# Splits moved to VectorE, a new order of slot widths, and exchanged operands in the last slot of a two-mixture kernel

## The chip, the core and the metric

The kernel runs on one core of a Trainium2 chip. Its engines work side by side and wait for one another through semaphores: PE (TensorE, matrix products), DVE (VectorE), ACT (ScalarE), POOL (GpSimd) and SP (SyncE, which here issues transfers); 16 DMA engines move data. The metric is the device time of one execution in microseconds (us). Unless another unit stands there, times in this text are us, and times within an execution count from the start of its span.

## The reference

All data are fp32. Attention comes first, then two mixtures of experts in a row, each with 1152 tokens of 512 values, 8 experts, and one expert per token:

```python
attn = softmax(scores + decay bias, causal) @ v      # 2 x 8 heads, 576 positions, 64 values
# mixture 1: at most `capacity` tokens of each expert are kept
e = argmax(x @ w_gate);  out = gate * (relu(x @ w1[e]) @ w2[e])      # w1 512x1024, w2 1024x512
# mixture 2: the same on that output, no capacity, a bias of each token's modality added to the logits
e = argmax(x @ w_gate2 + bias[modality]);  out = gate * (relu(x @ w1[e]) @ w2[e])
```

With the inputs used here the second mixture sends 550, 85 and 517 tokens to three experts and none to the others; the first mixture's experts 0 to 7 get 130, 137, 129, 143, 151, 156, 117 and 189.

## The kernel before

Attention fills about the first 110 us, with the routing of the first mixture at its end. The rest is a row of 13 *slots*. A slot is one expert with a fixed number of token columns. Slots 0 to 7 are the first mixture: slot 0 is expert 0 with 160 columns, slots 1 to 7 are the other experts sorted by their token count, and the widths stand in `WID` (160, 192, 168, 160, 152, 144, 136, 132). Slots 8 to 12 are the second mixture: 8 and 9 the expert with most tokens, 10 and 11 the second, with 276 columns each, and 12 a third with 92.

**Steps.** Every slot has eight steps j on PE, one for each 512 KB piece of weights. Steps 0 to 3 make 256 hidden rows each (`mul`, weights stationary, tokens moving), and relu follows in `fold` and `fold2`. Steps 4 to 7 make the output, 128 rows each; tiles of PSUM are shared by two steps. Where a slot is `native` (all of the first mixture but slot 1, and slot 12), PE multiplies fp32; each product shows as two matmul instructions in the trace. In slots 8 to 11 weights and tokens are split into a high and a low fp32r part and each product is three matmuls, hi x hi (L799), hi x lo (L800) and lo x hi (L801). Slot 1 is split too.

**Splits.** `split` (L697) makes the parts of a piece in two halves of 512 columns: ACT writes `hi`, and VectorE or GpSimd subtracts to give `lo`. With `alone` it is always VectorE; otherwise GpSimd takes the odd pieces. `stream` sets when a piece is fetched and split, in steps counted over all slots: in slot 8 (n = 8) piece i is fetched at step 57 + i and split at 60 + i, and used at 64 + i. Slot 10 is fetched and split later in the same manner; slots 9 and 11 use the parts of the slot before.

**The order around it.** PE's instructions are pinned in program order; SP's and POOL's transfers go out in order as well. `begin(prep(...))` starts a slot's transposes of gathered tokens (`ptx`, L760, to `xs` on ACT and VectorE) during the slot before, and `tail1` puts the routing of a finished slot among the next slot's products, at due times `T` (`TL` for slot 7) of a modelled clock: logits (`p`, `l`, `pl`, L882 to L894), the one-hot choice `oh` (L909), ranks by PE (`pr`, L912 to L915), then `place` (L154 to L183: `pos`, `colm`), the write of the slot's rows to DRAM (L941), and at the end the list of tokens by PE (`plist`, L944). For slot 7 this ends with `finished`: the list is read (L189) and POOL gathers the tokens of slot 9. `plan` (L1178 to L1194), which picks the experts of slots 10 to 12, comes between `place` and the write.

**The end.** Slot 12 goes the usual way: outputs with the 512 values on partitions are copied (`yT`, L843 and L844), turned by PE in two halves (`pty`, L866), scaled by ACT into `yr` (L867) and scattered to the output by POOL (L951), after a branch that would compute tokens left over (there are none here). `oi`, the rows to scatter to, comes from `tail2` (L962).

Of the kernel before, what the change touches and what calls it, by code (L numbers as in the profile page):

```python
# [26 lines left out]
GATE, TOK, BIAS = 512, 513, 520  # L27
NONE = 65536.0
OFF = {1: 2048, 2: 4096}
WID = [160, 192, 168, 160, 152, 144, 136, 132]  # L30
J1 = (N - H1) // H1 // W1 * W1 + W1 + 1
J2 = -(-(N + C2) // C2) * W2
J = {1: J1, 2: J2}
# [2 lines left out]
NSLOT2 = (N - E) // C2 + E  # L36
NS = {1: NOV, 2: NSLOT2}
PIECE = 1024
RAW = 8
T = 1.5, 2.3, 3.0, 5.6, 9.9, 2.0, 13.0  # L40
TL = 0.9, 1.7, 2.4, 4.6, 10.5, 2.0, 13.0
AWAKE = 22, 6, 16
DW = 128 + 2 * E
MID, PLACE = 32, 1.2
# [5 lines left out]
def shape_constants():  # L50

    import numpy as np

    p = np.arange(128).reshape(128, 1, 1)
    e = np.arange(E)
    tok = S * np.arange(B)[:, None] + 128 * np.arange(NT) - 64 + p
    tok[:, :, 0] = S * np.arange(B) + p[:, :, 0]
    t = {"io8": np.broadcast_to(e - E, (NT, E)), "tok": tok, "tok1": tok - OFF[1], "col": np.arange(E * J2),
         "row": C1 * np.arange(NCH)[:, None] + H1 * np.arange(W1) + p - OFF[2]}
    t["io8m"] = np.broadcast_to(t["io8"], (128, NT, E)).copy()  # L60
    t["io8m"][64:, 0, :] = 100
# [9 lines left out]
    t["width"] = np.array(WID[1:])  # L71
# [12 lines left out]

def build(tc, ctx, spots, tab, qk, v, s, wg, wa, cap, mod, wg2, mb, wb, out):
    nc = tc.nc
# [99 lines left out]

    def listed(dst, src, m):

        nc.vector.tensor_scalar_add(dst, src, float(OFF[m]))  # L189


    with ExitStack() as actx:
# [614 lines left out]
    def mul(k, j, lead=False):  # L807

        if j == 0:
            k.hs = (hidden1[:, 0:8 * k.c].rearrange("p (k c) -> p k c", k=8) if k.native else  # L810
                    hidden[:, 0:16 * k.c].rearrange("p (k s c) -> p k s c", k=8, s=2))
        if j == 4:
            k.yT = mp.tile([P, 4, k.c], F32, name="yT")
        if j < 4 or j % 2 == 0:
            k.ps = pg.tile([P, 2, 512], F32, tag="g", name="ps")
        if j < 4:
            for i in range(2):
                for kt in range(4):
                    if lead:
                        step(k)  # L820
                    product(k, k.ps[:, i], k.w[j], i * 512 + kt * P, k.xs[:, kt], kt == 0, kt == 3)
        else:
            late = j < 6 and k.two and 2 * k.c <= 512
            cuts = [(j, 0, 8)] if not late else [(4, 0, 4)] if j == 4 else [(5, 0, 4), (4, 4, 6), (5, 4, 6), (4, 6, 8), (5, 6, 8)]
            for d, k0, k1 in cuts:
                for kt in range(k0, k1):
                    if lead:
                        step(k)
                    product(k, k.ps[:, d % 2], k.w[d], kt * P, k.hs[:, kt], kt == 0, kt == 7)

# [28 lines left out]

    def back(k, yr, i):  # L860
        r0, r = k.rows[i]
        n = DM // P // (2 if k.last else 1)
        for d0 in range(0, DM // P, n):
            pt = pt_.tile([r, n * P], F32, tag="t", name="pty")
            for dt in range(n):
                pin(nc.tensor.transpose(pt[:, dt * P:(dt + 1) * P], k.yT[:, d0 + dt, r0:r0 + r], ident))  # L866
            nc.scalar.mul(yr[:r, i, d0 * P:(d0 + n) * P], pt, k.xc[:r, i, GATE:GATE + 1])  # L867
# [90 lines left out]
    def tail2(k):  # L958
        own = sm if k.last else mp
        oi = own.tile([H2, W2], I32, name="oi")  # L960
        with tc.issue_after(latest[nc.vector.engine]) if k.two else ExitStack():
            nc.vector.tensor_tensor(oi, k.xc[:, :, TOK], absent(k), op=ALU.add)  # L962
        yr = own.tile([H2, len(k.rows) if k.last else W2, DM], F32, name="yr2")
        for i in range(len(k.rows)):
            yield k.T[0] + (BRISK if k.next and k.next.last else T[5]) * i
            back(k, yr, i)
            if k.last:
                k.rest = lambda: put_rows(k, oi, yr, 0)
            else:
                put_rows(k, oi, yr, i)  # L970
# [70 lines left out]
    def when(t, f):  # L1041
        steps.setdefault(max(-(-t // 1), 0), []).append((t, f))

    def stream(n, k, src, known, pace=0.5):

        k.w, k.st = {}, {}

        def get(i):
            with tc.issue_after(k.hold()) if k.hold else ExitStack():
                k.st[i] = first[i] if n == 0 and i < len(first) else fetch(src, k.e, i)  # L1050

        def cut(i):
            k.w[i] = k.st.pop(i) if k.native else split(k.st.pop(i), i, alone=n < E)
        for i in range(8):
            tf = max(8 * n + i - FETCH, known + pace * i)
            ts = max(8 * n + i - SPLIT, tf + (2 if n < E else 3))
            when(tf, lambda i=i: get(i))
            when(ts, lambda i=i: cut(i))

    def ordered():  # L1060

        sq = [P, E - 1, E - 1]
        key = sm.tile([P, E - 1], F32, name="key")
        nc.vector.scalar_tensor_tensor(key, cnt1[:, 1:E], float(E), con["later"], op0=ALU.mult, op1=ALU.add)
        gt = sm.tile(sq, F32, name="gt")
        nc.vector.tensor_tensor(gt, key.unsqueeze(1).to_broadcast(sq), key.unsqueeze(2).to_broadcast(sq), op=ALU.is_gt)
        nth = sm.tile([P, E - 1], F32, name="nth")
        nc.vector.tensor_reduce(nth, gt, axis=AX.X, op=ALU.add)
        nc.vector.tensor_tensor(gt, nth.unsqueeze(1).to_broadcast(sq), col[:, 0:E - 1].unsqueeze(2).to_broadcast(sq),
                                op=ALU.is_equal)  # L1070
# [157 lines left out]
        nc.vector.tensor_tensor(done, done, full, op=ALU.min)  # L1228

    def finished():  # L1230
        listed(list2, pl2, 2)
        gather(seq[E + 1], pick(2, list2, seq[E + 1].cv))
        info["landed"] = nc.sync.dma_start(landed, seq[E + 1].xc[0:1, :, 0]).ins

    def assign():
# [7 lines left out]

    seq[E - 3].ranked = lambda: (choose(), close())
    seq[E - 3].listed = start
    seq[E - 1].placed = plan
    seq[E - 1].listed = finished
    at(E, KNOWN, assign)
    at(E + 1, 3, remain)
# [1 line left out]
    for i in range(5):  # L1251
# [16 lines left out]
    for n, k in enumerate(seq):  # L1268
# [13 lines left out]
            prev = (k, j)  # L1282
    finish()
    fold(*prev)
    for _ in k.tail():
        pass

    more_ = info["more"]
    latest.clear()
    with tc.If(more_ > 0):  # L1290
# [15 lines left out]
    k.rest()  # L1306


# [44 lines left out]
```

## Time and profile before

| | |
|---|---|
| median of 3 runs | 415.23 us (414.46 to 415.42) |
| the profiled execution | 418.99 us, its span 416.9 us |
| granted TensorE clock, mean | 0.99 of full speed |
| busy: PE, DVE, ACT, POOL | 398.1, 198.7, 179.6, 143.3 us |
| HBM read, written | 63.78, 10.51 MB |

The profile is one execution; it is 3.76 us longer than the median, of which 2.09 lie outside its span. An engine's busy time is the time in which it has an instruction at work; in a row of the timeline the first number is the start, the second the time that the merged instructions took, and brackets give the idle time ahead and what ended it.

### The profile page before, as it was taken

What the parts mean: (1) busy time and instruction counts of PE and PEld (TensorE: products, weight loads), DVE (VectorE), ACT (ScalarE), POOL (GpSimd) and SP (SyncE); (2) the same over time, 40 slices, a digit from 0 to 9 for tenths busy, and PEclk for the clock granted to TensorE, in tenths of its full rate; (3) what the DMA queues carried; (4) which work ended last, traced back from release to release, by engine and by line L of the source; (5) the groups of instructions that cost most, each with busy time, mean ns of one, the idle gap of its engine ahead of it and who ended that gap; (6) DMA issues with size and microseconds to landing.
All of it is one profiled execution on the core that took longest, in us unless ns stands there. A gap on an engine that the chain in (4) does not pass through costs nothing.

```text
span 416.9 us, 8847 instructions
## 1 busy us (share of the span) xinstructions
PE 398.1 (95%) x3177; PEld 367.2 (88%) x3177; DVE 198.7 (48%) x778; ACT 179.6 (43%) x472; POOL 143.3 (34%) x182
## 2 busy tenths in 40 slices
PE   8889999999889999999999999999999999999991
PEld 3778888888579999989899999989899999999990
DVE  8867779995715762314141423377721343221100
ACT  7979887896315632111211221266123454131221
POOL 4775876620281130302020202152556357030021
PEclk9999999999989999999999999999999999999997
DMA  4944896702138951767686878991059546010010
GB/s 175 313 134 156 313 380 231 266 4 85 45 110 300 375 179 39 237 205 263 203 265 211 270 239 270 266 343 53 8 170 375 169 152 190 36 31 27 0 51 23
DMA packets 30580, 74.64 MB, mean 179 GB/s; under 512 B 9196, under 2 KB 11628, under 8 KB 30526
## 3 DMA queue, kind: packets, MB, share of 16 engines
q1 hardware_dynamic: 24110, 66.72, 47.3%
q0 software_dynamic: 6336, 7.22, 6.6%
q8 instruction: 27, 0.44, 0.4%
q14 instruction: 27, 0.22, 0.2%
q10 hardware_dynamic: 80, 0.04, 0.0%
HBM read 63.78 MB, written 10.51 MB: 178 GB/s over the span
## 4 chain that ended last, share of the span: by engine, by line
PE 78%; DVE 9%; DMA 5%; ACT 3%; issue 1%; POOL 1%; POOLq 1%; SPq 0%; ACTq 0%; DVEq 0%
PE ps L791 30%; PE ps L799 6%; PE ps L800 6%; PE ps L801 6%; PE pt L365 5%; PE ps L365 5%; PE pty L866 3%; PE pb L365 3%; PE ps L795 2%; PE ptx L760 2%; PE px L365 2%; DMA wgid<-in_wg 2%; PE pa L365 2%; DVE lo L697 2%; PE p L882 1%
## 5 line engine op out<-in xcount | busy, mean ns | idle before, releaser
L791 PE MATMUL ps<-xn,st 128*128 128x160 f32 (+6 forms) x512 | 72.7, 296 | 0.4 <-ACT xn L779 0.4
L791 PE MATMUL ps<-hidden,st 128*128 128x160 f32 (+6 forms) x512 | 70.6, 292 | 0.0
L791 PEld LDWEIGHTS ps<-xn,st 128*128 128x128 f32 x512 | 67.8, 194 | 2.1 <-issue 1.0
L791 PEld LDWEIGHTS ps<-hidden,st 128*128 128x128 f32 x512 | 65.9, 190 | 0.6
L454 ACT ACTIVATE e<-sc,nmx 128x192 f32<-128x192 f32 (+4 forms) x80 | 44.7, 560 | 6.4 <-DVE sc L450 6.4
L844 DVE COPY yT<-ps 128x276 f32<-128x276 f32 (+7 forms) x24 | 8.5, 353 | 80.8 <-ACT yT L843 80.8
L721 POOL DMA_INDIRECT xc<-x,idx x14 | 15.0, 1074 | 75.1 <-DVE eq L904 54.7
L799 PE MATMUL ps<-xs,hi 128*128 128x276 f32 x128 | 38.4, 300 | 0.0
L799 PE MATMUL ps<-hidden,hi 128*128 128x276 f32 x128 | 38.2, 299 | 0.1
L843 ACT COPY yT<-ps 128x276 f32<-128x276 f32 (+7 forms) x24 | 7.6, 316 | 69.2 <-PE ps L791 39.3
L800 PE MATMUL ps<-hidden,hi 128*128 128x276 f32 x128 | 37.1, 289 | 0.2 <-DVE hidden L857 0.2
L800 PE MATMUL ps<-xs,hi 128*128 128x276 f32 x128 | 37.1, 290 | 0.0
L801 PE MATMUL ps<-xs,lo 128*128 128x276 f32 x128 | 37.1, 290 | 0.0
L801 PE MATMUL ps<-hidden,lo 128*128 128x276 f32 x128 | 37.1, 290 | 0.0
L365 PE MATMUL pt<-ident,e 128*128 128x128 f32 x240 | 35.4, 277 | 0.8 <-ACT e L454 0.6
L951 POOL DMA_INDIRECT out<-yr,oi x13 | 15.6, 1202 | 53.8 <-ACT yr L867 51.4
L697 POOL TENSOR_TENSOR lo<-st,hi 128x512 fp32r<-128x512 f32 x16 | 22.1, 1394 | 33.3 <-ACT hi L695 33.2
L450 DVE TENSOR_SCALAR_CACHE_REDUCE sc<-ps 128x192 f32<-128x192 f32 (+4 forms) x80 | 31.5, 417 | 2.0 <-ACT e L454 1.1
L365 PE MATMUL ps<-ka,qa 128*128 128x320 f32 (+2 forms) x96 | 30.0, 327 | 0.5 <-DVE sc L450 0.5
L695 ACT CAST hi<-st 128x512 fp32r<-128x512 f32 x48 | 27.7, 618 | 4.4 <-DMA st<-in_wa 3.5
L365 PEld LDWEIGHTS pt<-ident,e 128*128 128x128 f32 x240 | 26.1, 141 | 2.6 <-ACT e L454 0.8
L857 DVE SCALAR_TENSOR_TENSOR hidden<-ps,hidden 128x552 fp32r<-128x552 f32 x16 | 11.7, 731 | 29.7 <-ACT hidden L855 29.5
(292 smaller groups left out, 869.9 us busy)
## 6 DMA issues: line engine op xcount, KB each, us to landing
st<-in_wa SPq DMA_DIRECT2D x64, 512.0 KB
st<-in_wb SPq DMA_DIRECT2D x24, 512.0 KB
qkd<-in_qk SPq DMA_DIRECT2D x6, 1152.0 KB
y<-yr SPq DMA_DIRECT2D x8, 390.0 KB
vt<-in_v SPq DMA_DIRECT2D x8, 320.0 KB
qkd<-in_qk SPq DMA_DIRECT2D x4, 576.0 KB
out<-zrow SPq DMA_DIRECT2D x1, 2304.0 KB
x<-xrow SPq DMA_DIRECT2D x2, 768.0 KB
```

The costliest lines, as they stand in the source:

```text
L365: ins = op(*args, **kw)
L450: nc.vector.tensor_scalar(h.sc[t][:r, c0:c1], ps[:r, o0:o0 + c1 - c0], -0.125, low, op0=ALU.mult, op1=ALU.min, accum_out=h.nmx[t][:r])
L454: recent[:] = [nc.scalar.activation(ebuf[t, i][:r, :w], h.sc[t][:r, :w], AF.Exp, bias=h.nmx[t][:r], scale=-1.0, accum_out=rsum[:r, k.b, t, ...
L695: nc.scalar.copy(hi[:, c:c + h], st[:, c:c + h])
L697: eng.tensor_tensor(lo[:, c:c + h], st[:, c:c + h], hi[:, c:c + h].bitcast(F32), op=ALU.subtract)
L721: nc.gpsimd.indirect_dma_start(out=k.xc[:r, i, 0:rw], out_offset=None, in_=src, in_offset=bass.IndirectOffsetOnAxis(ap=idx[:r, i:i + 1], a ...
L791: pin(nc.tensor.matmul(out[:, 0:c], w[:, o:o + P], mv, start=first, stop=last, skip_group_check=True))
L799: pin(nc.tensor.matmul(out[:, 0:c], hi, mv[:, 0, :], start=first, stop=False, skip_group_check=True))
L800: pin(nc.tensor.matmul(out[:, 0:c], hi, mv[:, 1, :], start=False, stop=False, skip_group_check=True))
L801: pin(nc.tensor.matmul(out[:, 0:c], lo, mv[:, 0, :], start=False, stop=last, skip_group_check=True))
L866: pin(nc.tensor.transpose(pt[:, dt * P:(dt + 1) * P], k.yT[:, d0 + dt, r0:r0 + r], ident))
L951: put = nc.gpsimd.indirect_dma_start(out=out, out_offset=bass.IndirectOffsetOnAxis(ap=oi[:, i:i + 1], axis=0), in_=yr[:, i, :], in_offset= ...
```

## The change

1. The widths of slots 1 to 7 become 192, 136, 152, 132, 160, 144, 168 (ranks 0, 5, 3, 6, 2, 4, 1); each rank keeps its width.
2. The second weight matrix is packed in pieces of half of its 512 output values by half of its 1024 hidden rows. Steps 4 and 5 make the first 256 output rows, from hidden tiles 0 to 3 and 4 to 7, steps 6 and 7 the others. `late` cuts are gone.
3. Slot 8's pieces are split at steps 62 + i, all of them with VectorE; its `prep` begins at step 61, not 62.
4. `plan` is emitted after the gather of slot 9 and held behind the list; `TL[4]` is 9.4, not 10.5.
5. In slot 12's steps 4 to 7 the hidden tiles (128x92) are stationary and 256 weight columns move, so that tokens come out on partitions; ACT scales them straight into `yr`. Its `oi` is made at step 4, and its `tail2` is not run.

```diff
-WID = [160, 192, 168, 160, 152, 144, 136, 132]
+RANKED = [192, 168, 160, 152, 144, 136, 132]
+TURNS = [0, 5, 3, 6, 2, 4, 1]
+WID = [160] + [RANKED[r] for r in TURNS]
-TL = 0.9, 1.7, 2.4, 4.6, 10.5, 2.0, 13.0
+TL = 0.9, 1.7, 2.4, 4.6, 9.4, 2.0, 13.0
...
+        if j == 4 and k.last:
+            k.oi, k.yr = places(k), sm.tile([H2, 1, DM], F32, name="yrl")
...
-            late = j < 6 and k.two and 2 * k.c <= 512
-            cuts = [(j, 0, 8)] if not late else [(4, 0, 4)] if j == 4 else [(5, 0, 4), (4, 4, 6), (5, 4, 6), (4, 6, 8), (5, 6, 8)]
...
+            h, q = divmod(j - 4, 2)
+            if k.last:
+                for kt in range(4 * q, 4 * q + 4):
+                    for _ in range(2 if lead else 0):
+                        step(k)
+                    pin(nc.tensor.matmul(k.ps[:k.c, 0, 0:HD], k.hs[:, kt], k.w[j][:, kt % 4 * HD:kt % 4 * HD + HD],
+                                         start=kt == 0, stop=kt == 7, skip_group_check=True))
+                return
+            for k0 in range(4 * q, 4 * q + 4, 2 if j == 5 else 4):
+                for d in range(2):
+                    for kt in range(k0, k0 + (2 if j == 5 else 4)):
+                        if lead:
+                            step(k)
+                        product(k, k.ps[:, d], k.w[j], kt % 4 * HD + d * P, k.hs[:, kt], kt == 0, kt == 7)
...
+        if k.last and j > 3:
+            nc.scalar.mul(k.yr[:k.c, 0, HD * (j // 2 - 2):HD * (j // 2 - 1)], k.ps[:k.c, 0, 0:HD],
+                          k.xc[:k.c, 0, GATE:GATE + 1])
+            return
...
-            k.w[i] = k.st.pop(i) if k.native else split(k.st.pop(i), i, alone=n < E)
+            k.w[i] = k.st.pop(i) if k.native else split(k.st.pop(i), i, alone=n < E or i in late)
...
-            ts = max(8 * n + i - SPLIT, tf + (2 if n < E else 3))
+            ts = 8 * n + i - 2 if i in late else max(8 * n + i - SPLIT, tf + (2 if n < E else 3))
...
-        listed(list2, pl2, 2)
+        ready = listed(list2, pl2, 2)
         gather(seq[E + 1], pick(2, list2, seq[E + 1].cv))
+        with tc.issue_after(ready.ins):
+            plan()
...
-    seq[E - 1].placed = plan
...
-        at(n - 1, 7 if i == 1 else 6, lambda k=k, n=n: begin(prep(k, after=seq[n - 1])))
+        at(n - 1, (5, 7, 6, 6, 6)[i], lambda k=k, n=n: begin(prep(k, after=seq[n - 1])))
...
-            stream(n, k, wb, 8 * (E - 2) + 4) if i == 0 else stream(n, k, wb, 8 * (E + 1), 1)
+            stream(n, k, wb, 8 * (E - 2) + 4, late=range(8)) if i == 0 else stream(n, k, wb, 8 * (E + 1), 1)
```

## Rows read from the trace of the kernel before

**Rows 1.** The page: busy us of each engine (share of the span) x instructions.
```profile
PE 398.1 (95%) x3177; PEld 367.2 (88%) x3177; DVE 198.7 (48%) x778; ACT 179.6 (43%) x472; POOL 143.3 (34%) x182
```
**Rows 2.** Waits of PE: us in total, times, longest us.
```profile
PE ptx L760 <- DMA yc<-y,idx: 0.8, 1, 0.8
PE ptx L760 <- DVE xs L784: 0.7, 1, 0.7
...
PE pr L912 <- DVE oh L909: 0.4, 1, 0.4
```
**Rows 3.** Windows around the start of slot 8: us, busy by engine, clock, DMA, GB/s.
```profile
271.00:282.00 11.00, 10.31 (x93) 9.79 (x92) 8.33 (x20) 7.06 (x17) 5.49 (x4) 1.00 0.95 336
282.00:296.00 14.00, 13.73 (x113) 13.09 (x112) 11.81 (x41) 6.94 (x14) 6.04 (x4) 1.00 0.11 31
```
**Rows 4.** The chain that ended last, in slot 7: start, us, what.
```profile
265.62 5.39 DMA st<-in_wb
271.04 0.63 ACT hi L695
```
**Rows 5.** Timeline of PE, slots 7 and 8: start, us, instructions, idle before.
```profile
278.72 0.46 PE L760 MATMUL ptx<-ident,yc 92*128 92x92 f32 x3 [0.69 <-DVE xs L784]
...
288.57 0.17 PE L912 MATMUL pr<-oh,upper 96*96 96x16 bf16 x1
...
295.68 0.39 PE L944 MATMUL plist<-colm,pos 96*92 96x144 f32 x2 [0.27 <-DVE colm L183]
...
296.60 0.40 PE L799 MATMUL ps<-hidden,hi 128*128 128x276 f32 x1
...
299.46 0.39 PE L800 MATMUL ps<-hidden,hi 128*128 128x276 f32 x1 [0.19 <-DVE hidden L857]
...
307.37 0.30 PE L760 MATMUL ptx<-ident,yc 92*128 92x92 f32 x1 [0.75 <-DMA yc<-y,idx]
```
**Rows 6.** Timeline of POOL in slots 7 and 8.
```profile
273.54 2.93 POOL L697 TENSOR_TENSOR lo<-st,hi 128x512 fp32r<-128x512 f32 x2 [11.65 <-ACT hi L695]
...
291.47 2.06 POOL L697 TENSOR_TENSOR lo<-st,hi 128x512 fp32r<-128x512 f32 x1 [2.17 <-ACT hi L695]
294.00 1.31 POOL L697 TENSOR_TENSOR lo<-st,hi 128x512 fp32r<-128x512 f32 x1 [0.48 <-ACT hi L695]
```
**Rows 7.** Timeline of DVE in slots 7 and 8.
```profile
274.00 2.53 DVE L174 TENSOR_SCALAR pos<-ctab,pb__3761 96x92 fp32r<-96x92 f32 x2
...
277.03 1.28 DVE L697 TENSOR_TENSOR lo<-st,hi 128x512 fp32r<-128x512 f32 x2
...
284.90 0.22 DVE L894 TENSOR_REDUCE lg<-pl 96x16 f32<-96x64 f32 x1 [1.24 <-PE pl L889]
...
292.27 1.27 DVE L160 SCALAR_TENSOR_TENSOR pb__3993<-pb__3993,rank 96x2 f32<-96x2 f32 x1
293.58 0.56 DVE L174 TENSOR_SCALAR pos<-ctab,pb__3993 96x92 fp32r<-96x92 f32 x2
294.06 1.56 DVE L183 TENSOR_TENSOR colm<-ctab,hj 96x288 fp32r<-96x288 f32 x1
...
297.60 0.30 DVE L189 TENSOR_SCALAR list<-plist 92x144 int32<-92x144 f32 x1
```
**Rows 8.** Timeline of DVE in slot 1, whose splits VectorE makes alone.
```profile
142.59 0.22 DVE L894 TENSOR_REDUCE lg<-pl 96x16 f32<-96x64 f32 x1 [1.20 <-PE pl L889]
...
147.41 0.15 DVE L909 TENSOR_TENSOR oh<-ctab,mn 96x16 bf16<-96x16 f32 x1
```
**Rows 9.** Timeline: a native stretch of 168 columns, and the last slot's end.
```profile
168.30 3.67 PE L791 MATMUL ps<-xn,st 128*128 128x168 f32 x24
...
399.94 7.31 PE L791 MATMUL ps<-hidden,st 128*128 128x92 f32 x64
...
408.21 0.47 ACT L867 ACTIVATE yr<-pty,yc 92x256 f32<-92x256 f32 x1 [0.24 <-PE pty L866]
409.01 1.18 POOL L951 DMA_INDIRECT out<-yr,oi  x1 [8.23 <-ACT yr L867]
```

More of the change, by code (lines that the diff above doesn't have):

```diff
@@ L38 @@
 PIECE = 1024
+HD = DM // 2
 RAW = 8
 T = 1.5, 2.3, 3.0, 5.6, 9.9, 2.0, 13.0
-TL = 0.9, 1.7, 2.4, 4.6, 10.5, 2.0, 13.0
+TL = 0.9, 1.7, 2.4, 4.6, 9.4, 2.0, 13.0
 AWAKE = 22, 6, 16
@@ L70, in shape_constants @@
     t["base2"] = W[2] * np.arange(NS[2])
-    t["width"] = np.array(WID[1:])
+    t["width"] = np.array(RANKED)
+    t["turns"] = np.array(TURNS)
     t["later"] = E - 1 - np.arange(E - 1)
@@ L187, in listed @@
     def listed(dst, src, m):
-        nc.vector.tensor_scalar_add(dst, src, float(OFF[m]))
+        return nc.vector.tensor_scalar_add(dst, src, float(OFF[m]))
     with ExitStack() as actx:
@@ L811, in mul @@
                     hidden[:, 0:16 * k.c].rearrange("p (k s c) -> p k s c", k=8, s=2))
-        if j == 4:
+        if j == 4 and k.last:
+            k.oi, k.yr = places(k), sm.tile([H2, 1, DM], F32, name="yrl")
+        elif j == 4:
             k.yT = mp.tile([P, 4, k.c], F32, name="yT")
@@ L822, in mul @@
         else:
-            late = j < 6 and k.two and 2 * k.c <= 512
-            cuts = [(j, 0, 8)] if not late else [(4, 0, 4)] if j == 4 else [(5, 0, 4), (4, 4, 6), (5, 4, 6), (4, 6, 8), (5, 6, 8)]
-            for d, k0, k1 in cuts:
-                for kt in range(k0, k1):
-                    if lead:
-                        step(k)
-                    product(k, k.ps[:, d % 2], k.w[d], kt * P, k.hs[:, kt], kt == 0, kt == 7)
+            h, q = divmod(j - 4, 2)
+            if k.last:
+                for kt in range(4 * q, 4 * q + 4):
+                    for _ in range(2 if lead else 0):
+                        step(k)
+                    pin(nc.tensor.matmul(k.ps[:k.c, 0, 0:HD], k.hs[:, kt], k.w[j][:, kt % 4 * HD:kt % 4 * HD + HD],
[7 more added lines that the diff above has]
+                        product(k, k.ps[:, d], k.w[j], kt % 4 * HD + d * P, k.hs[:, kt], kt == 0, kt == 7)
     def fold(k, j):
@@ L861, in back @@
         r0, r = k.rows[i]
[L862 to L867, printed above, removed]
+        pt = pt_.tile([r, DM], F32, tag="t", name="pty")
+        for dt in range(DM // P):
+            pin(nc.tensor.transpose(pt[:, dt * P:(dt + 1) * P], k.yT[:, dt, r0:r0 + r], ident))
+        nc.scalar.mul(yr[:r, i, 0:DM], pt, k.xc[:r, i, GATE:GATE + 1])
     def absent(k):
@@ L956, in put_rows, with places, tail2 @@
         puts.append(put.ins)
-    def tail2(k):
-        own = sm if k.last else mp
-        oi = own.tile([H2, W2], I32, name="oi")
+    def places(k):
+        oi = (sm if k.last else mp).tile([H2, W2], I32, name="oi")
         with tc.issue_after(latest[nc.vector.engine]) if k.two else ExitStack():
             nc.vector.tensor_tensor(oi, k.xc[:, :, TOK], absent(k), op=ALU.add)
-        yr = own.tile([H2, len(k.rows) if k.last else W2, DM], F32, name="yr2")
+        return oi
+    def tail2(k):
+        oi = places(k)
+        yr = mp.tile([H2, W2, DM], F32, name="yr2")
         for i in range(len(k.rows)):
@@ L966, in tail2 @@
             back(k, yr, i)
[L967 to L970, printed above, removed]
+            put_rows(k, oi, yr, i)
     SP = mybir.EngineType.SP
@@ L1042, in when, with stream @@
         steps.setdefault(max(-(-t // 1), 0), []).append((t, f))
-    def stream(n, k, src, known, pace=0.5):
+    def stream(n, k, src, known, pace=0.5, late=()):
         k.w, k.st = {}, {}
@@ L1068, in ordered @@
         nc.vector.tensor_reduce(nth, gt, axis=AX.X, op=ALU.add)
-        nc.vector.tensor_tensor(gt, nth.unsqueeze(1).to_broadcast(sq), col[:, 0:E - 1].unsqueeze(2).to_broadcast(sq),
+        nc.vector.tensor_tensor(gt, nth.unsqueeze(1).to_broadcast(sq), con["turns"].unsqueeze(2).to_broadcast(sq),
                                 op=ALU.is_equal)
@@ L1284, in build @@
     fold(*prev)
-    for _ in k.tail():
-        pass
     more_ = info["more"]
@@ L1305, in build @@
         latest.clear()
-    k.rest()
+    put_rows(k, k.oi, k.yr, 0)
 def kernel(**inputs):
@@ L1316, in pack @@
         a = np.asarray(w1).reshape(E, 4, 128, 8, 128).transpose(0, 2, 3, 1, 4).reshape(E, 128, 4096)
-        c = np.asarray(w2).reshape(E, 8, 128, 4, 128).transpose(0, 2, 3, 1, 4).reshape(E, 128, 4096)
+        c = np.asarray(w2).reshape(E, 2, 4, 128, 2, HD).transpose(0, 3, 4, 1, 2, 5).reshape(E, 128, 4096)
         return np.concatenate([a, c], axis=2)
```

## The prediction

> **What bounds the kernel now.** I read the page's busy times first: PE is at work 95% of the span, no other engine half of it [rows 1]. So the time is PE's work, plus the stretches where PE stands still, plus what follows its last product. The widths of slots 1 to 7 have the same sum in either order, and the number of products is the same except in slot 12, so PE's work hardly moves; a gain has to come from stalls and from the end. The waits of PE are the second view: of those from slot 1 on, the two longest are one wait for slot 9's gathered rows and one for VectorE's part of slot 8's tokens [rows 2]. The windows and the timeline then say where: around the start of slot 8. VectorE, idle for half of the span, is at work 11.81 of the 14 us from 282 on, and from 271 to 282 the DMA engines are at work 95% of the time [rows 3]. In the timeline PE's idle times in slots 7 to 9 stand one by one: 0.69, 0.27, 0.19 and 0.75, together 1.90 [rows 5]. The chain of waits shows what the first hangs on: from 265.62 on a piece of slot 8's weights travels for 5.39, ACT makes its high part at 271.04, and VectorE's queue stands behind it [rows 4]. Last, the end: products until 399.94 + 7.31 = 407.25, the scatter's issue at 409.01 [rows 9].
>
> **The end (part 5 of the change).** Now 409.01 - 407.25 = 1.76 pass from the last product to the scatter, with copies, transposes and the second scaling of 0.47 in between. POOL starts 409.01 - 408.68 = 0.33 after that scaling ends [rows 9]. After the change one scaling of the same shape follows the last product directly: about 0.05 to its start (an estimate) + 0.47 + 0.33 = 0.85. Gain 0.9. The rows to scatter to are made at step 4, some 7 us ahead, beside PE's products; without that cover they would cost two short VectorE operations.
>
> The products themselves: 64 instructions of 92 columns take 7.31, 0.114 each. They become 32 of 256 columns, a width that no row shows. 168 columns take 3.67 / 24 = 0.153 each with the last one's drain [rows 9]. In proportion to columns that is 0.233, and 32 x 0.233 = 7.46 (0.15 more than now). Taking 0.31 off as the drain of the last one (an estimate, twice a mean spacing) leaves 3.36 / 23 = 0.146 each, so 0.2225 for 256 columns and 7.1 in all (0.2 less). I take 0, between close ends.
>
> **Slot 8's splits and prep (part 3).** Slot 8's first split moves from step 60 to 62, its transposes from step 62 to 61. VectorE's first `lo` then no longer stands ahead of them waiting for a piece that is still under way, and the 0.69 before the third group of transposes [rows 5] goes. What is late next is the ACT copy of the same tokens, which nothing delays. Slot 7 now has 168 columns and not 132, so the same weights have 168 / 132 = 1.27 times as long to arrive.
>
> The price is on VectorE. Pieces 1, 3, 5 and 7 were GpSimd's; they add 8 halves of 1.28 / 2 = 0.64 [rows 7], 5.1 in all. Against that stands what VectorE lost beside GpSimd. `pos` took 2.53 at 274.00 and 0.56 at 293.58. L160, an operation on two columns, took 1.27 and ended at 293.54, when GpSimd's half of 2.06 ended (293.53). `colm` took 1.56 from 294.06, beside a half that began at 294.00 and ended at 295.31 [rows 6, 7]. That is about 2.0 + 1.1 + 1.2 = 4.3 that comes back (the last two by what their time has beyond GpSimd's end or a few columns, an estimate). VectorE's time in the stretch thus grows by some 0.8, though it moves: pieces 2 to 7 are now all split inside slot 8.
>
> There it meets slot 7's routing. Before, `lg` starts at 284.90 and PE takes the ranks at 288.57, without a wait: 3.67 of room [rows 5, 7]. In slot 1, where VectorE makes all splits alone, the same chain takes 147.41 - 142.59 = 4.82 from `lg` to `oh` [rows 8], and PE waited 0.4 for it [rows 2]. So the new cost lies between 0 and 4.82 - 3.67 = 1.15; I take the measured 0.4. `plist` is due 1.1 of the modelled clock earlier, and its chain loses GpSimd's blocking but gets splits in between; I leave its wait at the 0.27 of today [rows 5], between 0 and 1.1.
>
> **Order of the second product (part 2).** In slots 8 to 11 step 4 needed hidden tiles 6 and 7 after 18 matmuls; now 36 come ahead. The wait of 0.19 for VectorE's hidden rows goes, and so does the stretching at step 4's first product (0.40 against 0.29 for its like, estimated at 0.1: its PSUM tile comes free with a VectorE operation that was late) [rows 5]. Native slots keep their sequence; only which piece a product reads changes, at no cost.
>
> **`plan` after the gather (part 4).** The list is written at 297.60, though `plist` ran at 295.68 and took 0.39; VectorE did `plan` and a relu in between [rows 5, 7]. The gathered rows came 0.75 too late for PE [rows 5]. With `plist` 1.1 earlier on the clock and `plan` behind it, the list should stand over 1.5 earlier against PE's products: the 0.75 goes. Queues behind: POOL issues slot 9's three gathers and then slot 10's; SP holds slot 10's weights until slot 9's rows have landed, so they start earlier too. `plan` itself now ends later, but its result is read at step 70 for rows and weights used at step 80.
>
> **Widths (part 1).** Wide and narrow slots alternate, where three narrow ones stood last. No wait of PE for a transfer of weights stands in the view of [rows 2], so I give this nothing beyond the time that slot 7 gains.
>
> **Sum.** 0.90 + 0.69 + 0.19 + 0.11 + 0.75 - 0.40 = 2.24. The profiled execution took 418.99 and would take 416.75; against the median of 415.23 that is 413.0. The forecast's own range: all waits gone with no new one, and faster last products, 0.90 + 0.69 + 0.27 + 0.30 + 0.75 + 0.2 = 3.1 (412.1); a new wait of 1.15 and slower products, 2.64 - 1.15 - 0.15 = 1.3 (413.9).
>
> **Rivals.**
> - *Only the end is shorter.* Around slot 8 each wait that goes makes room for another of the same size: VectorE still does the tail, the splits and the relus in one queue. For it: VectorE's load there is as high as before. Against: two of the waits hang on things that the change takes apart (a late piece, `plan` ahead of the list). Gain 0.9: 414.3. The case that the new order of emission doesn't reach the engines' queues is in it.
> - *VectorE becomes the bound in slot 8* (slower). If the long `pos`, L160 and `colm` were not GpSimd's doing, nothing comes back: then the window's 11.81 [rows 3] grows by four more halves net (eight for pieces 2 to 5, where about four ran before), 2.6, to 14.4 of 14, and pieces 4 to 7 come late. If each holds PE for one whole split of 1.28, that is 5.1, and the result is 415.23 - 2.24 + 5.1 = 418.1. It decides from the point where VectorE has no idle time left in steps 64 to 67. Against it: two operations ended with GpSimd's pieces to within 0.3.
>   The Trainium skill speaks for this rival on the page "Perfetto Trace Analysis", section "Optimizing Scalar/DVE Operations": with VectorE saturated, work may be moved off it, even to GpSimd; the change does the reverse. The same section warns that the two share an SBUF port, so that moving between them may not help, and "SBUF — State Buffer", section "Who interferes with whom", calls that port an exclusive lock for operations of two SBUF inputs. By the first rule the time is 418.1, by the lock it is the forecast; L160's end with GpSimd's piece agrees with the lock.
> - *The order of widths gives more.* The DMA engines are busy 95% of 271 to 282 [rows 3]; if other transfers of the stretch, gathers and row writes, also come earlier, another 1.5 of small waits (the rest of PE's 1.90 and the plist wait, twice over at most) could go: about 411.5. Against: PE stands still for little else.
>
> **How the numbers follow.** Forecast 0.64, only the end 0.19, VectorE the bound 0.09, more from the order 0.08. A measurement here tells about 0.3%, 1.25, from no change. Faster is the first and the last, 0.72; within 0.3% the second, 0.19; slower 0.09. The predicted time is 413.0; the range runs from 411.4 (the last rival) to 415.2, where the second case and unfavourable parts of the forecast end.
>
> **What would show it.** The end: the scatter's issue some 0.85 after the last product, no `pty` for slot 12. Slot 8: no L697 on POOL before slot 10, no `xs` wait of the transposes, `pos` and `colm` near 0.5; a wait of `pr` for `oh` of up to 1.15. Slot 9: no wait of the transposes for gathered rows. It is wrong if `lo` of slot 8 shows among PE's waits, if slots 2 or 4, now narrow, wait for weights, or if the last slot's products take over 7.5.

## The result

The changed kernel takes 411.33 us (median of 6 runs, 411.18 to 411.65), the kernel before 415.07 in the runs beside it. The ratio is 0.9901, with a 95% interval of 0.9877 to 0.9925: faster, by 3.74 us in the medians. The sign was forecast, the size was not: 2.24 us were predicted, and 411.33 lies just below the range (411.4 to 415.2).

Timed runs of the kernel before lie between 414.46 and 418.0. Much of that comes from ahead of slot 1: in two profiles of it (418.99 and 414.62 us) slot 0 ends at 138.16 and at 134.30. So parts of the change are compared on one *stretch* of the profile: from the end of slot 0 (the first `p` on PE) to the issue of the last scatter on POOL. It is the same to within 0.2 us in two profiles of one kernel: 409.01 - 138.16 = 270.85 before [rows 9] and 402.23 - 135.13 = 267.10 after. The gain there is 3.75 us.

The page of the changed kernel: busy us of each engine.

```profile
PE 395.5 (97%) x3141; PEld 363.0 (89%) x3141; DVE 198.4 (48%) x784; ACT 178.6 (44%) x470; POOL 133.1 (33%) x174
```

PE works 2.6 us less than in [rows 1], but most of that is chance: the second profile of the kernel before has 395.9. POOL works 10 less, and VectorE the same, though it makes eight more halves of splits. The windows of [rows 3] in the changed kernel (slot 8 begins at 277.06 instead of 281.18):

```profile
271.00:282.00 11.00, 11.00 (x86) 10.13 (x85) 7.51 (x19) 5.57 (x13) 0.00 (x0) 1.00 0.56 181
282.00:296.00 14.00, 14.00 (x114) 13.81 (x113) 13.06 (x52) 7.83 (x15) 3.00 (x3) 1.00 0.13 33
```

The windows show no idle time of PE any more, though VectorE is at work for 13.06 of 14 us. The timeline of PE, the lines of [rows 5] with the line ahead of some:

```profile
271.24 0.78 PE L795 MATMUL ps<-hidden,st 128*128 128x168 f32 x4
271.86 0.40 PE L764 MATMUL ptx<-ident,yc 92*128 92x92 f32 x3
...
284.57 0.17 PE L927 MATMUL pr<-oh,upper 96*96 96x16 bf16 x1
...
289.60 0.29 PE L805 MATMUL ps<-xs,lo 128*128 128x276 f32 x1
289.86 0.39 PE L959 MATMUL plist<-colm,pos 96*92 96x144 f32 x2
...
292.05 0.29 PE L803 MATMUL ps<-hidden,hi 128*128 128x276 f32 x1
...
301.17 0.75 PE L764 MATMUL ptx<-ident,yc 92*128 92x92 f32 x3
```

No bracket of idle time is left here. Two waits without a bracket remain: a group of transposes of slot 9's rows takes 0.75 instead of 0.40, so one of its three waited within the group, 0.35 of the former 0.97; and `plist` still waits 0.21 (next section). A third, 0.31 at the first products of slot 9, stands in both kernels. The timeline of VectorE, the lines of [rows 7]:

```profile
265.76 0.56 DVE L178 TENSOR_SCALAR pos<-ctab,pb__3760 96x92 fp32r<-96x92 f32 x2
...
280.89 0.22 DVE L909 TENSOR_REDUCE lg<-pl 96x16 f32<-96x64 f32 x1 [0.60 <-PE pl L904]
...
282.54 0.17 DVE L924 TENSOR_TENSOR oh<-ctab,mn 96x16 bf16<-96x16 f32 x1
...
288.68 0.16 DVE L164 SCALAR_TENSOR_TENSOR pb__3981<-pb__3981,rank 96x2 f32<-96x2 f32 x1
...
289.35 0.45 DVE L187 TENSOR_TENSOR colm<-ctab,hj 96x288 fp32r<-96x288 f32 x1
...
291.56 0.30 DVE L193 TENSOR_SCALAR list<-plist 92x144 int32<-92x144 f32 x1
```

Nothing is stretched any more: the `pos` that took 2.53 takes 0.56, L160, now L164, 0.16 instead of 1.27, `colm` 0.45 instead of 1.56. The list is read 291.56 - 277.06 = 14.50 us after slot 8's start; before it was 297.60 - 281.18 = 16.42. The end, the lines of [rows 9]:

```profile
394.35 7.07 PE L834 MATMUL ps<-st,hidden 128*92 128x256 f32 x32
...
401.46 0.47 ACT L850 ACTIVATE yrl<-ps,yc 92x256 f32<-92x256 f32 x1 [2.98 <-PE ps L834]
402.23 1.18 POOL L966 DMA_INDIRECT out<-yrl,oi  x1 [7.04 <-ACT yrl L850]
```

The products take 7.07 instead of 7.31, and 402.23 - 401.42 = 0.81 pass to the scatter instead of 1.76.

### The profile page after: what moved, and what is told of

Its sections match the earlier page's. It is cut to its first block, busy times and chain, and to the rows that moved or that the text cites. A ratio compares the mean times of both kernels' runs of the same rounds, so it can differ in the third digit from the quotient of the medians.

```text
span 409.6 us, 8766 instructions
## 1 busy us (share of the span) xinstructions
PE 395.5 (97%) x3141; PEld 363.0 (89%) x3141; DVE 198.4 (48%) x784; ACT 178.6 (44%) x470; POOL 133.1 (33%) x174
## 4 chain that ended last, share of the span: by engine, by line
PE 81%; issue 7%; DVE 6%; ACT 2%; DMA 1%; POOL 1%; POOLq 0%; DVEq 0%; ACTq 0%
PE ps L795 29%; PE ps L803 7%; PE ps L804 7%; PE ps L805 7%; PE pt L369 6%; PE ps L369 5%; PE pb L369 3%; PE pty L881 3%; PE ps L799 3%; PE ptx L764 2%; PE pa L369 2%; PE px L369 2%; PE p L897 2%; DMA out<-yr,oi 1%; PE awake L152 1%
## 5 line engine op out<-in xcount | busy, mean ns | idle before, releaser
L795 PE MATMUL ps<-xn,st 128*128 128x160 f32 (+6 forms) x512 | 71.0, 291 | 0.4 <-ACT xn L783 0.4
L795 PEld LDWEIGHTS ps<-xn,st 128*128 128x128 f32 x512 | 66.2, 190 | 2.0 <-issue 0.9
L795 PE MATMUL ps<-hidden,st 128*128 128x160 f32 (+5 forms) x448 | 62.9, 294 | 0.0
L795 PEld LDWEIGHTS ps<-hidden,st 128*128 128x128 f32 x448 | 58.5, 190 | 0.5
L861 DVE COPY yT<-ps 128x276 f32<-128x276 f32 (+6 forms) x22 | 8.0, 362 | 68.3 <-ACT yT L860 68.1
L860 ACT COPY yT<-ps 128x276 f32<-128x276 f32 (+6 forms) x22 | 7.1, 322 | 58.1 <-PE ps L795 30.6
L701 DVE TENSOR_TENSOR lo<-st,hi 128x512 fp32r<-128x512 f32 x40 | 27.3, 705 | 6.3 <-ACT hi L699 6.2
L966 POOL DMA_INDIRECT out<-yr,oi x12 | 14.4, 1201 | 45.7 <-ACT yr L882 43.3
```

The source lines that it names most:

```text
L701: eng.tensor_tensor(lo[:, c:c + h], st[:, c:c + h], hi[:, c:c + h].bitcast(F32), op=ALU.subtract)
L795: pin(nc.tensor.matmul(out[:, 0:c], w[:, o:o + P], mv, start=first, stop=last, skip_group_check=True))
L966: put = nc.gpsimd.indirect_dma_start(out=out, out_offset=bass.IndirectOffsetOnAxis(ap=oi[:, i:i + 1], axis=0), in_=yr[:, i, :], in_offset= ...
```

## Measure of a wait

A bracket shows PE idle from the modelled end of one matmul to the next start. But a matmul of 276 columns lasts 0.29 and the next one starts after 0.13, so an undisturbed PE overlaps them; a wait costs its bracket and the lost overlap. What it costs is seen *end to end*: the end of a line less the end of the line ahead, against the same pair undisturbed. The kernel before, in slots 7 and 8, lines that stand around those of [rows 5]:

```profile
275.54 1.32 PE L791 MATMUL ps<-hidden,st 128*128 128x132 f32 x10
276.70 0.40 PE L760 MATMUL ptx<-ident,yc 92*128 92x92 f32 x3
276.94 1.10 PE L791 MATMUL ps<-hidden,st 128*128 128x132 f32 x8
...
295.12 0.29 PE L801 MATMUL ps<-xs,lo 128*128 128x276 f32 x1
...
296.20 0.29 PE L801 MATMUL ps<-xs,lo 128*128 128x276 f32 x1
...
298.99 0.28 PE L799 MATMUL ps<-hidden,hi 128*128 128x276 f32 x1
```

Undisturbed transposes end 277.10 - 276.86 = 0.24 after the products ahead. The disturbed ones ended 279.18 - 278.04 = 1.14 after them: the bracket of 0.69 cost 0.90. In the same way the first product of step 4 cost 0.51 - 0.13 = 0.38, the wait for hidden tiles 299.85 - 299.27 - 0.13 = 0.45, and slot 9's rows 307.67 - 306.61 - 0.09 = 0.97. For `plist` the second profile of the kernel before (e0) has an undisturbed pair:

```profile
291.25 0.29 PE L801 MATMUL ps<-xs,lo 128*128 128x276 f32 x1
291.38 0.31 PE L944 MATMUL plist<-colm,pos 96*92 96x144 f32 x2
```

It takes 291.69 - 291.54 = 0.15. In the first profile it took 296.07 - 295.41 = 0.66, so its bracket of 0.27 cost 0.51. In the changed kernel it takes 0.36, and begins 0.06 after `colm` ends at 289.80: it still waits 0.21 for VectorE, with no bracket to show it. The change takes 0.30 off.

## The experiments

e0 and e11 are the two kernels once more; the others are the changed kernel with an edit. Stretch: from profiles, as above. Medians and ratios against the kernel before are of timed runs; their intervals reach 0.2 to 0.4% to either side, so between these variants the stretch tells more.

| kernel | stretch | median | ratio to before |
|---|---|---|---|
| before | 270.85 | 415.07 | |
| e0, before again | 270.68 | 414.62 (1 run) | |
| changed | 267.10 | 411.33 | 0.9901 (0.9877 to 0.9925) |
| e11, changed again | 266.90 | 410.55 | 0.9893 (0.9873 to 0.9913) |
| e1, old end | 267.80 | 412.49 | 0.9923 (0.9898 to 0.9947) |
| e2, old widths | 267.31 | 411.24 | 0.9888 (0.9868 to 0.9908) |
| e3, GpSimd splits | 267.21 | 411.40 | 0.9894 (0.9875 to 0.9914) |
| e4, early splits | 266.57 | 410.89 | 0.9885 (0.9864 to 0.9907) |
| e5, old widths, early splits | 268.27 | 411.69 | 0.9896 (0.9852 to 0.9940) |
| e6, plan ahead | 266.83 | 410.94 | 0.9884 (0.9844 to 0.9925) |
| e7, three pieces at once | 266.96 | 410.92 | 0.9886 (0.9846 to 0.9926) |
| e8, GpSimd splits, plan ahead | 268.63 | 412.06 | 0.9924 (0.9901 to 0.9947) |
| e9, old order of products | 266.91 | 410.47 (1 run) | |
| e10, early and paced | 265.92 | 410.38 | 0.9892 (0.9871 to 0.9912) |

**e0 and e11: both kernels once more.**

> The kernel before once more, for a second profile. My theory: the stretch from the end of slot 0 (the first p of the timeline) to the scatter's issue is fixed by the program and comes out at 270.85 again to within 0.3, and the three us by which the first profile reached that point later than the changed kernel's (138.16 against 135.13) are chance, so this one gets there near 135. Rival: the changed kernel is earlier there as well, for a reason in attention; then 138 again.

The kernel before, second profile, timeline of PE and POOL:

```profile
134.30 0.47 PE L882 MATMUL p<-yT,wg2s 128*32 128x160 f32 x4
...
404.98 1.18 POOL L951 DMA_INDIRECT out<-yr,oi  x1 [8.23 <-ACT yr L867]
```

The stretch repeats, and slot 0 ends at 134.30, so the first profile's late start was not the kernel's doing. Inside the stretch two things differ: `plist` found its operands in time and the first product of step 4 behind it waited 0.89 (0.51 and 0.38 in the first profile, the same sum), and slot 9's rows cost 0.77 instead of 0.97.

> The changed kernel once more beside these, for its time on this chip and a second profile: 267.1 from slot 0's end to the scatter to within 0.4, the part that may differ being the landing of slot 9's rows (0.34 in the first profile).

As expected; the rows of slot 9 came 0.35 late again.

**e1: the old end.**

```diff
-            if k.last:
-                for kt in range(4 * q, 4 * q + 4):
...
-        if k.last and j > 3:
-            nc.scalar.mul(k.yr[:k.c, 0, HD * (j // 2 - 2):HD * (j // 2 - 1)], k.ps[:k.c, 0, 0:HD],
...
+    for d0 in (0, 2):
...
+            pin(nc.tensor.transpose(pt[:, dt * P:(dt + 1) * P], k.yT[:, d0 + dt, 0:k.c], ident))
+        nc.scalar.mul(k.yr[:k.c, 0, d0 * P:d0 * P + HD], pt, k.xc[:k.c, 0, GATE:GATE + 1])
```

> Slot 12 goes the old way again (weights stationary, copies, transposes in two halves, scaling), all else as changed. My theory: the end is worth what the two profiles show, 7.31 against 7.07 for the products and 1.76 against 0.80 from the last product to the scatter's issue, so 1.2 us slower than the changed kernel (412.5). Rival: the scatter's landing and what follows, 7.89 against 7.37 in the two profiles, belong to the end as well, then 1.7 slower (413.0).

The end of that kernel:

```profile
393.83 7.31 PE L795 MATMUL ps<-hidden,st 128*128 128x92 f32 x64
...
402.10 0.47 ACT L1293 ACTIVATE yrl<-pty,yc 92x256 f32<-92x256 f32 x1 [0.24 <-PE pty L1292]
402.90 1.18 POOL L953 DMA_INDIRECT out<-yrl,oi  x1 [8.23 <-ACT yrl L1293]
```

7.31 and 402.90 - 401.14 = 1.76 are back, 1.19 together. The stretch is only 0.7 to 0.9 longer, since in this profile slot 9's rows cost 0.08 and not 0.35; the timed median is 1.2 to 1.9 above the two of the changed kernel. What follows the scatter took 7.50. In the eleven profiles with the new end (two of the changed kernel, nine of its variants) it took 7.2 to 7.6 (spans are read to 0.1), so the old end adds nothing there and the rival is not borne out.

**e2 and e5: the widths, and the widths with early splits.**

```diff
-TURNS = [0, 5, 3, 6, 2, 4, 1]
+TURNS = [0, 1, 2, 3, 4, 5, 6]
# e5 also:
-            ts = 8 * n + i - 2 if i in late else max(8 * n + i - SPLIT, tf + (2 if n < E else 3))
+            ts = max(8 * n + i - SPLIT, tf + (2 if n < E else 3))
```

> Widths 192, 168, 160, 152, 144, 136, 132 again, all else as changed. My theory: the late splits alone already keep VectorE from waiting for a piece under way (it landed near 271, the first split is then at about 275), so the order of widths is worth 0 to 0.2 us. Rival: the wide slot 7 is what took away the wait of slot 8's transposes for xs, which cost 0.91 from one matmul's end to the next; then 0.9 or more slower (412.2), with that wait back in the trace.

In e2 the third group of slot 8's transposes, which had the bracket of 0.69 before, comes without one; 0.2 to 0.4 us of stretch are lost:

```profile
273.20 0.40 PE L764 MATMUL ptx<-ident,yc 92*128 92x92 f32 x3
```

> Old widths and splits at steps 60 + i, VectorE alone, all else as changed: the two runs that undid one of these had no xs wait, so here both are undone. My theory: either of the two keeps VectorE from waiting for a piece under way, and without both the wait of slot 8's transposes comes back with 0.5 to 0.9 from end to end of a matmul. Rival: GpSimd's blocking of pos (2.53) made that wait; then none here.

The chain of waits in e5, and the third group of transposes in its timeline of PE:

```profile
263.69 6.35 DMA st<-in_wb
...
270.06 0.63 ACT hi L699
...
270.71 0.69 DVE lo L701
```

```profile
273.20 1.09 PE L795 MATMUL ps<-hidden,st 128*128 128x132 f32 x8
275.57 0.46 PE L764 MATMUL ptx<-ident,yc 92*128 92x92 f32 x3 [1.27 <-DVE xs L788]
```

With both edits undone the wait is back: a piece of slot 8's weights lands at 270.04, its `lo` stands ahead of the transposes' copy in VectorE's queue, and PE loses 276.03 - 274.29 - 0.24 = 1.50, more than the 0.5 to 0.9 expected. The stretch is 1.2 to 1.4 longer than that of the changed kernel. VectorE made all splits here and `pos` took 0.55, so a late piece makes such a wait without GpSimd. But e5 does not restore the kernel before: it keeps the earlier transposes (2.4 us earlier against slot 8's start), and piece 1, GpSimd's before, now stands in VectorE's queue. In the kernel before, the chain of [rows 4] goes on through the stretched `pos` to the halves of piece 2, which stand ahead of the transposes' copy and end at 278.31. ACT had their `hi` parts sooner:

```profile
275.67 1.14 ACT L695 CAST hi<-st 128x512 fp32r<-128x512 f32 x2
```

With a `pos` of 0.56 those halves could have ended near 277.5 (an estimate: `hi` until 276.81 and one half of 0.69), which would leave little of the 0.90. So the rival, GpSimd's hold on `pos`, is not excluded there; no run separates the two. Neither e2 (late splits with the old widths) nor e4 (early splits with the wide slot 7) has the wait: in the changed kernel's company each of the two edits alone removes it.

**e3: half of the splits on GpSimd again.**

```diff
-            k.w[i] = ... split(k.st.pop(i), i, alone=n < E or i in late)
+            k.w[i] = ... split(k.st.pop(i), i, alone=n < E)
```

> GpSimd takes the odd pieces of slot 8 again, at the late steps, all else as changed. My theory: GpSimd blocks VectorE again; pos, L164 and colm are stretched beyond 1 us, plist waits 0.5, and the list and slot 9's rows come later: 0.8 to 1.6 us slower (412.1 to 412.9). Rival: VectorE is relieved by eight halves of 0.64 and nothing else is late: no change, or up to 0.5 faster.

The timelines of POOL and VectorE (slot 8 begins at 277.67):

```profile
288.08 2.04 POOL L701 TENSOR_TENSOR lo<-st,hi 128x512 fp32r<-128x512 f32 x1 [2.19 <-ACT hi L699]
```

```profile
288.86 1.27 DVE L164 SCALAR_TENSOR_TENSOR pb__3981<-pb__3981,rank 96x2 f32<-96x2 f32 x1
...
291.66 0.30 DVE L193 TENSOR_SCALAR list<-plist 92x144 int32<-92x144 f32 x1
```

The two-column operation on VectorE takes 1.27 again and ends at 290.13, with GpSimd's half (290.12). `pos` and `colm` behind it are not stretched (0.56 and 0.45). `plist` waits 0.88 end to end, 0.67 more than in the changed kernel. Yet the list stands 13.99 after slot 8's start, sooner than the 14.50 of the changed kernel, and slot 9's rows come in time, 0.35 less: the stretch is only 0.1 to 0.3 longer. My theory of a loss of a microsecond falls. The hold is real and paid for at `plist`, but here the gathered rows of slot 9 then cost nothing, which gives back half of it.

**e6: `plan` ahead of the list.**

```diff
-TL = 0.9, 1.7, 2.4, 4.6, 9.4, 2.0, 13.0
+TL = 0.9, 1.7, 2.4, 4.6, 10.5, 2.0, 13.0
...
-        with tc.issue_after(ready.ins):
-            plan()
...
+    seq[E - 1].placed = plan
```

> plan ahead of the list and TL[4] = 10.5 again, all else as changed. My theory: the list is read 1 to 2 us later against slot 8's start (it was 16.07 after it before, 14.10 in the changed kernel), and PE waits for slot 9's rows 0.8 to 1.8 longer than in the changed kernel (0.34 there from end to end): 412.2 to 413.1. Rival: GpSimd's blocking alone made the list late; then within 0.3 us of the changed kernel.

VectorE's timeline (slot 8 begins at 278.35):

```profile
290.65 0.45 DVE L187 TENSOR_TENSOR colm<-ctab,hj 96x288 fp32r<-96x288 f32 x1
291.02 0.16 DVE L1193 SCALAR_TENSOR_TENSOR keyp<-run,ctab 128x8 f32<-128x8 f32 x1
...
293.01 0.30 DVE L193 TENSOR_SCALAR list<-plist 92x144 int32<-92x144 f32 x1
```

The theory falls again: the list stands 14.66 after slot 8's start, 0.16 later than in the changed kernel, and slot 9's rows cost 0.21. (The expectation counts from slot 8's first product, 0.35 to 0.4 behind the start used here.) `colm` is ready at 12.75 of the slot, and `plan` (`keyp` is its first operation) then runs while `plist` waits in PE's queue for its turn. Ahead of the list it cost nothing here, where VectorE was on time.

**e8: e3 and e6 together.**

> Both undone at once: GpSimd takes slot 8's odd pieces and plan stands ahead of the list with TL[4] = 10.5, all else as changed. Undone alone, neither made PE wait longer for slot 9's rows. My theory: GpSimd pushes colm back by 0.7 us and plan then comes between plist and the list, as before; the list is read 15.5 to 16.5 us after slot 8's start and PE waits again for the rows, 0.5 to 1.4 from end to end; the stretch from slot 0's end to the scatter is 267.6 to 268.6. Rival: each is worth nothing in either company, and the rows came late before because of something else (the early splits); then within 0.3 of 267.1.

The timelines of POOL, VectorE and PE (slot 8 begins at 276.25):

```profile
289.20 1.67 POOL L701 TENSOR_TENSOR lo<-st,hi 128x512 fp32r<-128x512 f32 x1 [0.51 <-ACT hi L699]
```

```profile
287.45 1.27 DVE L164 SCALAR_TENSOR_TENSOR pb__3981<-pb__3981,rank 96x2 f32<-96x2 f32 x1
...
289.60 1.29 DVE L1193 SCALAR_TENSOR_TENSOR keyp<-run,ctab 128x8 f32<-128x8 f32 x1
...
292.74 0.30 DVE L193 TENSOR_SCALAR list<-plist 92x144 int32<-92x144 f32 x1
```

```profile
291.79 0.40 PE L803 MATMUL ps<-hidden,hi 128*128 128x276 f32 x1 [0.60 <-DVE hidden L874]
...
302.55 0.30 PE L764 MATMUL ptx<-ident,yc 92*128 92x92 f32 x1 [1.20 <-DMA yc<-y,idx]
```

Together they bring the old state back. The list stands 292.74 - 276.25 = 16.49 after the slot's start, against 16.42 before the change and 14.0 to 14.7 with either edit alone. Slot 9's rows cost 1.41 end to end, step 4's first product 0.87. The stretch is 1.5 to 1.7 longer, at the upper end of what was expected. `keyp`, eight columns, takes 1.29 instead of the 0.16 of e6 and ends at 290.89, as GpSimd's half does (290.87). So VectorE's lateness took both: time lost beside GpSimd, and `plan` in the queue.

**e9: the old order of the second product.**

```diff
+            if j < 6 and 2 * k.c > 512:
+                for kt in range(8):
...
+                    product(k, k.ps[:, q], k.w[4 + kt // 4], kt % 4 * HD + q * P, k.hs[:, kt], kt == 0, kt == 7)
+                return
```

> In slots 8 to 11 steps 4 and 5 make one output tile each over all eight hidden tiles, as before, with the new weight packing, all else as changed. My theory: slot 8's PE waits for hidden tiles 6 and 7 again, 0.3 to 0.5 from end to end (0.46 before), and nothing else moves. Rival: that wait came from VectorE's lateness and not from the order; then none here.

The timelines of PE and VectorE in e9, in step 4 of slot 8, and VectorE's in the kernel before:

```profile
293.53 0.29 PE L805 MATMUL ps<-hidden,lo 128*128 128x276 f32 x1
```

```profile
292.24 0.73 DVE L880 SCALAR_TENSOR_TENSOR hidden<-ps,hidden 128x552 fp32r<-128x552 f32 x1 [0.24 <-ACT hidden L878]
```

```profile
298.69 0.72 DVE L857 SCALAR_TENSOR_TENSOR hidden<-ps,hidden 128x552 fp32r<-128x552 f32 x1
```

The line of 293.53 is the eighteenth of the step. PE goes on to hidden tile 6 without a wait: VectorE wrote it by 292.97, 1.6 after the step's first product (291.38). Before the change it took until 299.41, 2.8 after that product at 296.60 [rows 5]. The stretch is that of the changed kernel (266.91 against 266.90 in e11). The theory falls: the order alone is worth nothing once VectorE is on time. e8, where VectorE is late and the order new, has no such wait at the hidden tiles either, so again either is enough.

**e7: three pieces at the start of one step.**

```diff
-            ts = 8 * n + i - 2 if i in late else ...
+            ts = (8 * n if 2 <= i <= 4 else 8 * n + i - 2) if i in late else ...
```

> Pieces 2, 3 and 4 of slot 8 are all split at step 64, the others as changed. It asks why PE did not wait for oh, for which I had put down 0.4. My theory: splits enter VectorE's queue at the start of a step, step 64 lasts 5 us with slot 7's routing in it, and only one piece was split there, so the chain from lg to oh ran unbroken (280.89 to 282.71); with three pieces it is cut by up to four halves of 0.64 and pr waits 0.2 to 1.0. Rival: the chain keeps its place whatever stands in the step, and pr waits for nothing.

The timelines of VectorE and PE, where slot 7's routing meets slot 8's splits:

```profile
280.79 1.28 DVE L701 TENSOR_TENSOR lo<-st,hi 128x512 fp32r<-128x512 f32 x2
...
284.53 0.17 DVE L924 TENSOR_TENSOR oh<-ctab,mn 96x16 bf16<-96x16 f32 x1
```

```profile
284.75 0.21 PE L927 MATMUL pr<-oh,upper 96*96 96x16 bf16 x1 [0.25 <-DVE oh L924]
```

As the theory had it: from the start of `lg` (280.65) to the end of `oh` are 4.05, against 282.71 - 280.89 = 1.82 in the changed kernel, and `pr` waits 0.46 end to end. Pieces enter VectorE's queue where a step begins. In the changed kernel one enters per step, ahead of or behind the chain and not within it. The stretch is no longer for it (266.96): `plist` does not wait, the list came sooner (14.11) and the rows of slot 9 cost nothing.

**e4 and e10: a version that might be faster.** e4 takes only slot 8's late splits back (the edit to `ts` shown with e5). e10 has that edit too, and

```diff
-TH = 1.5, 2.3, 3.0, 6.6, 10.9, 2.0, 14.2
+TH = 1.5, 2.3, 3.0, 7.1, 10.9, 2.0, 14.2
...
-                yield (1.0 * kp if after else 0.0)
+                yield ((0.69 if k is seq[E + 1] else 1.0) * kp if after else 0.0)
```

> Slot 8's pieces are split at steps 60 + i again, by VectorE alone, all else as changed. My theory: with 168 columns in slot 7 the pieces land in time, so no wait comes back, and four halves leave slot 8 for slot 7, where VectorE is idle: within 0.3 us of the changed kernel, with plist no later. Rival: the first split stands ahead of the transposes' VectorE part again, and xs waits 0.7 to 0.9 (412.1).

> A version meant to be faster: splits of slot 8 at steps 60 + i by VectorE (266.56 from slot 0's end to the scatter), the ranks of slot 0 taken later (TH[3] 7.1 for 6.6) since pr waits 0.57 from end to end there in every run so far, and slot 9's four groups of transposes closer together (0.69 for 1.0), since its first products wait 0.31 for xs. My theory: both waits shrink to under 0.1 and the stretch is 265.6 to 265.9, 1.2 us under the changed kernel. Rival: the waits move to the next operation in line (ranks of slot 0 late for the list, transposes waiting for slot 9's rows or a PSUM tile) and the stretch stays at 266.5.

The list in e4 (slot 8 begins at 277.05), in VectorE's timeline:

```profile
290.95 0.30 DVE L193 TENSOR_SCALAR list<-plist 92x144 int32<-92x144 f32 x1
```

13.90 after the slot's start instead of 14.50, the transposes of slot 9 do not wait (0.40 at 301.16), and the stretch is 0.33 to 0.53 shorter, as expected. In e10 the first rank product of slot 0 (0.17 at 143.97, no bracket) and slot 9's first products also lose their waits. Its stretch is 265.92, 1.0 to 1.2 below the changed kernel's. Timed beside e11 on one chip it has 410.38 against 410.55, with ratios of 0.9892 and 0.9893. In the profile it is shorter; that it is faster is not shown.

## Why the prediction was wrong

The terms of the sum, as predicted and as measured end to end in the stretch (before and changed, first profiles):

| term | predicted | measured |
|---|---|---|
| end, last product to scatter | 0.90 | 0.95 |
| the last products | 0 | 0.24 |
| wait of slot 8's transposes (`xs`) | 0.69 | 0.90 |
| hidden tiles, first product of step 4 | 0.19 + 0.11 | 0.45 + 0.38 |
| slot 9's rows | 0.75 | 0.97 - 0.35 = 0.62 |
| `plist` | 0 | 0.30 |
| `pr` | -0.40 | 0 |
| sum | 2.24 | 3.84 |

The gain of the stretch is 3.75; the rest of it loses the 0.1. The timed medians differ by 3.74. In e0 `plist` and the first product of step 4 share their 0.68 of gain otherwise, as said there.

**The failed step is the sizing of the wait terms in the sum.** I put down three waits of [rows 5] by their brackets and the first product of step 4 by its stretching (0.11). A bracket counts from the modelled end of the matmul ahead and leaves out the overlap that PE loses besides, 0.21 to 0.26 a wait here, `plist` included; the first product lost 0.27 more than I gave it. The four waits that I had as gone were 1.74 in the sum and are 2.35 (2.70 but for the 0.35 by which slot 9's rows were late in both profiles of the changed kernel). **A second step failed beside it, the 0.40 for `pr`,** taken from slot 1, where pieces enter in the midst of the chain. Here one enters per step, and the room of 3.67 stayed ample; e7 has the cost that I feared, 0.46, with three pieces at once. The wait of `plist`, left at its size, shrank as well (0.30), and the last products came out at the favourable end of my bounds (0.24; 7.07 / 32 = 0.221 each). These four make 1.55 of the 1.60 that lacked; the end gave the rest. That the time fell outside the range, and not just inside, is small beside this: 0.07, less than the 0.16 by which the median of the kernel before moved (415.23, then 415.07).

**The mechanisms.** *The end*: as predicted, 0.81 where I had 0.85, and e1 brings 1.19 back with the products. *Slot 8's splits*: a late piece does make an `xs` wait (e5's chain), but how much of the 0.90 was its and how much GpSimd's hold on `pos` is open. Late splits weren't needed against it; the wide slot 7, to which I gave only "the time that slot 7 gains", does it alone (e4). *The order of products*: the wait went, but not for the reason that I gave. VectorE, no longer late, has the tiles ready in either order (e9). *`plan`*: the rows came sooner, but `plan` behind the list was not what did it alone (e6); it takes `plan` ahead and GpSimd's halves together to make the list late (e8).

**VectorE.** The price came out much as worked out: eight halves more, and a busy time over the execution that does not grow (198.7 and 198.4), since `pos`, L160 and `colm` are short again. 13.06 of 14 us are busy and PE waits only the 0.21 at `plist`, so the rival of VectorE as the bound fell. e3 and e8 show GpSimd's hold three times, to within 0.02 us (L164 in both, `keyp` in e8). The rule of the Trainium skill, "SBUF — State Buffer", section "Who interferes with whom", that the shared port is an exclusive lock for operations of two SBUF inputs, agrees with these rows; the advice of "Perfetto Trace Analysis", section "Optimizing Scalar/DVE Operations", to move work off a full VectorE even to GpSimd, brings nothing here: e3 does so and is no faster. The warning of that section, that the two share a port and the move may not help, agrees with e3.

**The other rivals.** "Only the end" falls: with the last products it is 1.19, and 2.56 of the 3.75 lie elsewhere. "The order of widths gives more" gave the right size (411.5) by luck: undoing the widths alone costs 0.2 to 0.4 (e2), and its 1.5 does not follow from the rows that it names. After the waits that the forecast takes off, 0.27 of PE's 1.90 is left, `plist`'s, and twice that is 0.54. The range ended near this rival's time, 0.07 above what was measured, because my own best case, 3.1, was also counted in brackets.

Open: what follows the scatter took 7.89 and 7.62 in the two profiles of before and 7.37 and 7.36 in those of the changed kernel. e1, with the old end, has 7.50, so the end does not make the difference; what does is not shown.

## What to carry to other kernels

Price a wait by the distance from end to end against an undisturbed pair, not by the idle time that stands beside it; for PE's overlapping products the two differed by some 0.2 here. When several edits aim at one late queue, undo them in pairs too: four of the waits here have two edits that each remove them, and either one undone alone looks nearly worthless. And see that the pair undone is the old state: e5 was not. Work put on an engine that is nearly full cost little where it entered ahead of or behind a due chain. Where it entered within, the chain grew from 1.82 to 4.05 (e7), and PE paid only what went beyond the chain's room, 0.46.

## What the runs showed of the hardware

A VectorE operation on 8 columns was held until GpSimd's half had ended, 1.29 for 0.16 (e8), and one on 2 columns, 1.27 for 0.16 (e3, e8): so small an operation waits out the rest of GpSimd's like a wide one. A second fact is of the transposes of a slot's rows, in two row groups: 96 and the rest. Each line here merges four of them, two of either group. They are slot 2's rows, in slot 1, in the changed kernel (136 columns: 96 and 40) and in the kernel before (168 columns: 96 and 72):

```profile
151.67 0.58 PE L764 MATMUL ptx<-ident,xc 96*128 96x96 f32 x4
```

```profile
154.72 0.46 PE L760 MATMUL ptx<-ident,xc 96*128 96x96 f32 x4
```

The next product begins 0.51 and 0.26 after them; with two such lines in the slot that is the whole difference of slot 1, which lasts 22.57 instead of 22.07. Of the widths from 132 to 168 only 168 has the short form, in both kernels (0.46); the others take 0.57 to 0.61. So the new order moves the long form into slot 1 and the short one into slot 6, where the slot of 168 columns is prepared now. What makes the difference was not tried.
